# One TensorE block for a unit's gate products, and wider planned margins for float64 conversions

## The chip, the cores and the metric

The kernel runs on one core of a Trainium2 chip, in one launch. The metric is the device time of that launch in microseconds (us). Engines are named as in the profile: PE is TensorE (PEld its weight loads), DVE is VectorE, ACT is ScalarE, POOL is GpSimd, and SP is SyncE, which here only issues DMA transfers. Every engine works through its own instructions strictly in the order in which they were written; an instruction that has to wait holds up all that stand behind it on that engine.

## What is computed

Three computations follow each other. The first is an attention with a window of 16 positions and, beside it, one summary key (a maximum) and one summary value (a mean) for each block of 32 positions. The second is a mixture of 8 experts with a fixed capacity, where tokens are given to experts by their sorted gate logits. The third is a bilinear feed-forward network. The reference, cut to what matters:

```python
q, k, v: (4, 8, 768, 64)                       # float32
scores = [where(|i-j| < 16, q k^T / 8, -1e9),  q k_blockmax^T / 8 + log 32]
x = softmax(scores) @ [v, v_blockmean]         # -> x: (3072, 512)

logits = x @ w_gate                            # (3072, 8): the gate
# tokens go to experts in order of falling logits, 384 tokens to each expert
h = maximum(x[mask_e] @ w1[e], 0);  x[mask_e] = h @ w2[e]      # 8 experts

out = (((x @ wa) * (x @ wb)) @ w3) @ w_out     # wa, wb: (512, 1024); w3: (1024, 1024)
```

The weights wa, wb, w3 and w_out of the third part arrive as float64, of which the chip's engines read the two 32-bit halves; everything else is float32.

## The kernel before

**Stages.** In the attention stage, 16 units (a batch element and two heads each) are worked off with three groups each, 48 groups in all. A group makes scores on PE, subtracts the maximum (DVE, POOL), takes the exponential (ACT), transposes (PE), multiplies with the values (PE) and normalises (DVE). Its output `xo` is transposed on PE and copied by ACT to a tile `xt` of 128 x 256, and `xt` is multiplied with the gate weights `wg` (the gate product, PE, 32 output rows into a quarter of the PSUM tile `rt`, L755 to L763). Four units of a batch element add up in one `rt`; its sum is copied to `lt`, transposed and put into the logits `LG` (L764 to L771). Beside this work, the attention stage converts w_out and w3. When the last logits are there, the routing of expert 0 starts, which is a search in six rounds on DVE with small matmuls on PE (`key`, `gq`, `need`, `base`), and the products w3 x w_out are made on PE (`fold`: `ac<-wh,xh` and the like). After that come the 8 experts, about 93 us each; expert 0's stretch also converts wa and wb and holds the routing of expert 1. An expert has four layers: l1 and l2 are the expert's two matrices, l3 the bilinear products with wa and wb (`ab` tiles), l4 the product with the folded matrix.

**A conversion.** `conv` (L564 to L582) turns 128 x 512 float64 numbers into float32. SP loads them into `st` (one of two buffers, 512 KB) or, for the first halves of wa and wb, into an `ab` tile. Then ACT takes the magnitude of the high words (`a<-st`) and converts the low words in place (`st<-st`); DVE does three instructions (two TENSOR_SCALAR `a<-a`, one SCALAR_TENSOR_TENSOR `a<-st,a`); POOL adds (`a<-a,st` or `w<-a,st`), and with that the `st` buffer is free again. For w_out, ACT and POOL then split the result into `wh` and `wl`; for wa and wb, ACT and POOL split it into two `ab` tiles. There are 40 conversions: 24 are due in the attention stage, 8 in expert 0's routing, 8 in the beginning of expert 0.

**What sets the order.** The kernel isn't written in the order in which it runs. Class `Plan` (L100 to L323) records every instruction with its engine, its due time (`with at(t)`) and an estimated duration, and `Plan.run` (L221 to L323) lists them engine by engine: it goes forward in an estimated time, and whenever an engine is free it takes the ready instruction with the earliest due time. An instruction is ready when its operands are done, plus a margin where they come from another engine: 200 ns in general (SAFE_O), 1200 ns when PE reads them (SAFE_A), and 1500 ns more behind a DMA load (SAFE_D). Instructions recorded after the attention's buffers are given up (`late`; the 16 conversions of wa and wb among them) get no margin, save 600 ns for PE. The margins are not in the program that runs; they only push an instruction further back in its engine's order. `with nc.block()` makes several PE instructions one entry of the plan, so that nothing is put between them. Otherwise every instruction is an entry of its own, and PE's entries are chosen with a malus when the array's tiling changes (PEN, SWITCH); a gate product uses 128 rows by 32 columns of the array, most of its neighbours all 128 columns.

Before the change, gate products are recorded singly, each with its own operands; those of units 0 and 1 of a batch element are recorded together after unit 1, those of units 2 and 3 after unit 3, for the last batch element unit by unit and at last group by group. All recorded code runs through L380, so line numbers say little, and instructions are told apart by their tiles.

Of the kernel before, what the change touches and what calls it, by code (L numbers as in the profile page):

```python
# [99 lines left out]
class Plan:  # L100
# [3 lines left out]
    def __init__(self, nc):  # L104
        self.nc, self.ops, self.base, self.t, self.hot = nc, [], 0, 0.0, False
        self.hots, self.dma = set(), 0.0
        self.gate, self.bar, self.late = None, None, []
        self.rings, self.free, self.done, self.last, self.grabbed = {}, {}, {}, {}, ()
        self.clock, self.ctx = 0.0, nullcontext
        self.parts, self.modes, self.mode = None, {}, None  # L110
        for e in ("tensor", "vector", "scalar", "gpsimd", "sync"):
            setattr(self, e, Engine(self, e))
# [7 lines left out]
    @contextmanager  # L120
    def urgent(self):

        self.hot, old = True, self.hot
        yield
        self.hot = old

    @contextmanager
    def low_precision(self, reason):
# [22 lines left out]
    def add(self, eng, fn, reads, writes, dur, post):  # L151
        i = len(self.ops)
        deps, bufs = {}, []
        for v, wr in [(v, False) for v in reads] + [(v, True) for v in writes]:
            b = v.buf
            for j, kj, wj in b.seen:
                if j != i and (wr or wj) and overlap(v.key, kj):
                    deps[j] = max(deps.get(j, 0), 2 if wj and not wr else 1)
            if b not in bufs:
                bufs.append(b)  # L160
                b.uses += 1
        for v, wr in [(v, False) for v in reads] + [(v, True) for v in writes]:
            if not v.buf.seen or v.buf.seen[-1] != (i, v.key, wr):
                v.buf.seen.append((i, v.key, wr))
        for v in self.grabbed:
            bufs.append(v.buf)
            v.buf.uses += 1
        self.grabbed = ()
        if self.gate is not None:
            deps.setdefault(self.gate, 0)  # L170
        if any(b.pool is p for b in bufs for p in self.late if len(p) < 1 or b.n > 1):
            deps.setdefault(self.bar, 0)
        new = [b for b in bufs if not b.held]
        for b in bufs:
            if b.held and b.first is not None:
                deps.setdefault(b.first, 0)
        for b in new:
            b.held, b.first = True, i
            if b.fifo:
                if b.ring in self.last:  # L180
                    deps.setdefault(self.last[b.ring], 0)
                self.last[b.ring] = i
        deps.pop(i, None)
        if self.hot:
            self.hots.add(i)
        self.ops.append((eng, fn, deps, bufs, new, self.t, dur, post))

    def whole(self, tile, shape):
# [32 lines left out]
    def run(self):  # L221
# [22 lines left out]
        while todo:  # L244
            moved = False
            for e, (wait, q) in ready.items():
# [42 lines left out]
                for j in users.get(i, ()):  # L289
                    kind = ops[j][2][i]  # L290
                    if kind == 0:
                        settle(i, j, t)
                    else:
                        late = self.bar is not None and j > self.bar
                        safe = 0.0
                        if e != ops[j][0] and not late:
                            safe = SAFE_A.get(ops[j][0], SAFE_O) + (SAFE_D if post else 0.0)
                        elif e != "tensor" and ops[j][0] == "tensor":
                            safe = SAFE
                        settle(i, j, done + safe + (0.0 if post else LAG[e].get(ops[j][0], 0.0)))  # L300
            if moved:
                continue
# [27 lines left out]
       "gpsimd": {"tensor": 143, "scalar": 76, "vector": 80, "sync": 240}}  # L330

HOLD = 150.0

SWITCH, PEN = 150.0, 3.0

# [96 lines left out]
def body(tc, q, k, v, w_gate, w1, w2, wa, wb, w3, wo, out):  # L432
# [131 lines left out]
    def conv(src, r, h, dst, t, raw=None):  # L564

        with at(t - P_CL):
            raw = stage() if raw is None else raw
            nc.sync.dma_start(raw.bitcast(I32), src[r * 128:(r + 1) * 128, h * 512:(h + 1) * 512].bitcast(I32))
        with at(t):
            w = raw.bitcast(I32).rearrange("p (a b) -> p a b", b=2)  # L570
            lo, hi = w[:, :, 0], w[:, :, 1]
            c = ep.tile([128, 512], F32, name="a", bufs=3)
# [12 lines left out]
    for j in range(FB):  # L585
        t = P_C0 + (T0 - P_C1) * j / nconv
        f = conv(wo, j, 0, None, t)
        with at(t):
            WO[j] = wu()
            split_sb(WO[j][0], WO[j][1], f)  # L590
            for x in WO[j]:
                nc.keep(x)
# [99 lines left out]
    def group(G):  # L692
# [59 lines left out]
            nc.scalar.activation(xt, ps, AF.Copy)  # L752
            XT[u, g] = xt

        last = b == B - 1 and pr == HP - 1  # L755
        for x in ([(u, g)] if last else [(y, i) for y in (u - 1, u) for i in range(3)] if g == 2 and (pr == 1 or pr == 3)
                  else [(u, i) for i in range(3)] if g == 2 and b == B - 1 and pr == 2 else []):
            with at(STEP * G + P_SC):
                y, i = x
                if y % HP == 0 and i == 0:  # L760
                    GT[b] = pp.tile([128, 256], F32, name="rt", fifo=True)
                nc.tensor.matmul(GT[b][32 * i:32 * i + 32], WG[:, y % HP], XT[x].rearrange("p t s -> p (t s)"),
                                 start=(y % HP == 0), stop=(y % HP == HP - 1))  # L763
        if pr == HP - 1 and g == 2:  # L764
            with at(STEP * G + P_SC):
                lt = ap_.tile([96, 256], F32, name="lt", bufs=1)
# [499 lines left out]
```

## Time and profile before

| | us |
|---|---|
| median of 3 runs | 1042.55 |
| lowest and highest | 1041.95, 1046.04 |
| the profiled execution | 1044.22 |
| its span, first to last instruction | 1042.4 |
| PE busy (share of the span) | 955.7 (92%) |
| DVE busy | 662.1 (64%) |
| ACT busy | 406.1 (39%) |
| POOL busy | 322.4 (31%) |

The profiled execution lies 1.7 us over the median, and 1.8 us of it lie outside its span. The busy shares are averages over stages that are limited by different things, so they have to be read by stage: a table of stretches gives each engine's busy time, PE's granted clock and the DMA engines' share. What an engine waited for stands in a list of waits (summed), in the timeline (each instruction with the idle time before it in brackets), and in the chain of waits, which goes back from the last instruction and at each step to what released it.

### The profile page before, as it was taken

Reading aid. Unit: us, or ns where it says so; the run is one execution under the profiler, and the core shown is the slowest. Engines: PE = TensorE matmul, PEld = TensorE weight load, DVE = VectorE, ACT = ScalarE, POOL = GpSimd, SP = SyncE. Lnnn points to the kernel's source line nnn. Section 1 sums busy time; section 2 is a strip of 40 time slices with the busy share of each in tenths; the row PEclk is TensorE's granted clock in tenths of the full one; section 3 lists DMA queues with packets and bytes.
Section 4 is the critical chain, followed back from the end, with each engine's and each line's share of the span. In section 5 each row is a group of like instructions: output and inputs, shape, how many; then the busy total and the mean of one; then the engine's idle time right before and its main releaser. Section 6 shows DMA issues by size and latency. Waiting matters only on the chain.

```text
span 1042.4 us, 17312 instructions
## 1 busy us (share of the span) xinstructions
PE 955.7 (92%) x6339; PEld 847.5 (81%) x6339; DVE 662.1 (64%) x1992; ACT 406.1 (39%) x845; POOL 322.4 (31%) x393
## 2 busy tenths in 40 slices
PE   5799977997688899999999999999999999999995
PEld 4577766765477789979988997998899799999994
DVE  6989978879978972882686288258628825423210
ACT  4778866745244333232323323232332323323211
POOL 8877757525613631030121103012110304101001
PEclk9999999999889899999999999999999999999998
DMA  8999987570323331040113105011310405101000
GB/s 222 222 262 237 227 207 185 149 246 1 129 66 99 121 105 58 1 162 11 52 66 98 60 2 162 11 51 66 98 60 1 162 11 172 41 11 51 1 1 31
DMA packets 84007, 102.12 MB, mean 98 GB/s; under 512 B 31185, under 2 KB 64465, under 8 KB 83921
## 3 DMA queue, kind: packets, MB, share of 16 engines
q1 hardware_dynamic: 70864, 54.86, 19.7%
q0 software_dynamic: 13056, 46.14, 13.4%
q8 instruction: 50, 0.82, 0.3%
q14 instruction: 37, 0.30, 0.1%
HBM read 86.00 MB, written 12.58 MB: 95 GB/s over the span
## 4 chain that ended last, share of the span: by engine, by line
PE 61%; DVE 17%; issue 11%; DMA 6%; ACT 3%; SPq 1%; POOL 1%; POOLq 0%; DVEq 0%; ACTq 0%
PE mm L380 35%; PE ac L380 24%; DVE a L380 4%; DVE gq L380 2%; PE rt L380 2%; DMA st<-in_moe_w_dram 2%; DVE s L380 1%; DMA qn<-in_q_dram 1%; SPq L380 1%; DMA vn<-in_v_dram 1%; DVE xl L380 1%; DMA vw<-in_v_dram 1%; DMA st<-in_moe_w_out_dram 1%; DVE wl L380 1%; DVE kw L380 1%
## 5 line engine op out<-in xcount | busy, mean ns | idle before, releaser
L380 PE MATMUL mm<-xh,ab 128*128 128x384 f32 x1024 | 275.8, 341 | 0.0
L380 PEld LDWEIGHTS mm<-xh,ab 128*128 128x128 f32 x1024 | 188.4, 190 | 4.2 <-issue 2.6
L380 PE MATMUL mm<-xl,ab 128*128 128x384 f32 x512 | 175.7, 343 | 1.9 <-DVE xl L380 1.9
L380 DVE TENSOR_TENSOR a<-a,mm 128x384 f32<-128x384 f32 x64 | 35.3, 551 | 143.5 <-PE mm L380 120.9
L380 PE MATMUL ac<-w,hh 128*128 128x512 f32 x384 | 124.6, 400 | 0.0
L380 PEld LDWEIGHTS mm<-xl,ab 128*128 128x128 f32 x512 | 97.2, 190 | 4.7 <-DVE xl L380 3.2
L1056 POOL DMA_INDIRECT ra<-in_moe_w_dram,iw x32 | 31.7, 991 | 200.3 <-DVE go L380 190.9
L380 ACT ACTIVATE a<-mm 128x384 f32<-128x384 f32 x64 | 31.4, 491 | 147.3 <-PE mm L380 130.5
L380 PE MATMUL mm<-xh,wh 128*128 128x384 f32 x256 | 88.0, 345 | 0.4 <-ACT xh L380 0.4
L380 PE MATMUL ac<-hl,wh 128*128 128x384 f32 x256 | 87.1, 340 | 0.0
L380 PE MATMUL mm<-xl,wh 128*128 128x384 f32 x256 | 86.9, 339 | 0.0
L380 PE MATMUL mm<-xh,wl 128*128 128x384 f32 x256 | 86.8, 339 | 0.0
L380 PE MATMUL ac<-hh,wl 128*128 128x384 f32 x256 | 86.5, 338 | 0.0
L380 PE MATMUL ac<-hh,wh 128*128 128x384 f32 x256 | 84.1, 337 | 0.0
L1118 POOL DMA_INDIRECT out_dram<-a,idx x24 | 26.7, 1113 | 176.9 <-ACT a L380 173.6
L380 DVE TENSOR_TENSOR wl<-st,wh 128x512 fp32r<-128x512 f32 x64 | 45.5, 711 | 56.1 <-ACT wh L380 55.8
L380 PEld LDWEIGHTS ac<-w,hh 128*128 128x128 f32 x384 | 70.8, 188 | 11.6
L380 ACT ACTIVATE hh<-a 128x384 fp32r<-128x384 f32 x64 | 33.6, 525 | 119.3 <-DVE a L380 117.2
L1056 POOL DMA_INDIRECT xg<-xd,idx x24 | 25.3, 1054 | 167.4 <-PE mm L380 128.2
L380 PE MATMUL ac<-w,hl 128*128 128x512 f32 x192 | 76.6, 399 | 0.0
L380 ACT ACTIVATE wh<-ra 128x512 fp32r<-128x512 f32 x64 | 41.9, 666 | 65.5 <-PE mm L380 30.7
L380 DVE TENSOR_TENSOR wl<-ra,wh 128x512 fp32r<-128x512 f32 x64 | 43.9, 688 | 31.7 <-ACT wh L380 31.7
(253 smaller groups left out, 2096.2 us busy)
## 6 DMA issues: line engine op xcount, KB each, us to landing
st<-in_moe_w_dram SPq DMA_DIRECT2D x24, 512.0 KB, 3.9
kn<-in_k_dram SPq DMA_DIRECT2D x32, 192.0 KB, 4.8
qn<-in_q_dram SPq DMA_DIRECT2D x32, 192.0 KB, 4.1
vn<-in_v_dram SPq DMA_DIRECT2D x8, 768.0 KB, 9.2
xd<-xo SPq DMA_DIRECT2D x48, 128.0 KB, 4.1
vw<-in_v_dram SPq DMA_DIRECT2D x32, 176.0 KB, 4.7
st<-in_moe_w_out_dram SPq DMA_DIRECT2D x8, 512.0 KB, 5.2
ab<-in_moe_w_dram SPq DMA_DIRECT2D x8, 512.0 KB, 8.0
```

The costliest lines, as they stand in the source:

```text
L380: return getattr(real_engine, method)(*map(real, a), **{k: real(x) for k, x in kw.items()})
L1056: nc.add("gpsimd", lambda: tc.nc.gpsimd.indirect_dma_start(out=real(dst), out_offset=None, in_=real(src), in_offset=bass.IndirectOffsetOnA ...
L1118: s = tc.nc.gpsimd.indirect_dma_start(out=out, out_offset=bass.IndirectOffsetOnAxis(ap=real(idx), axis=0), in_=real(o), in_offset=None)
```

## The change

It has three parts. (1) A unit's three gate products are recorded as one block after its third group, for every unit, and so is the accumulation over the four units; no unit is paired with another any more. (2) `nc.patient()` marks instructions, those of SP excepted; `conv` uses it for its six instructions behind the load, and the split of w_out for its two. (3) For a marked instruction the planner's margin behind another engine is at least 1000 ns (CALM), and behind a DMA load 3500 ns (CALM_D); for instructions recorded after the attention's buffers are given up it is 0.3 of that, 300 and 1050 ns.

```diff
@@ Plan.__init__
+        self.calm, self.calms = False, set()
@@ class Plan
+    @contextmanager
+    def patient(self):
+
+        self.calm, old = True, self.calm
+        yield
+        self.calm = old
@@ Plan.add
+        if self.calm and eng != "sync":
+            self.calms.add(i)
@@ Plan.run, where an instruction i is done and its user j becomes ready
                         elif e != "tensor" and ops[j][0] == "tensor":
                             safe = SAFE
+                        if j in self.calms and e != ops[j][0]:
+                            safe = max(safe, (CALM_D if post else CALM) * (0.3 if late else 1.0))
                         settle(i, j, done + safe + (0.0 if post else LAG[e].get(ops[j][0], 0.0)))
@@
+CALM, CALM_D = 1000.0, 3500.0
@@ conv, behind its load
-        with at(t):
+        with at(t), nc.patient():
@@ the split of w_out
-        with at(t):
+        with at(t), nc.patient():
             WO[j] = wu()
@@ group
-        last = b == B - 1 and pr == HP - 1
-        for x in ([(u, g)] if last else [(y, i) for y in (u - 1, u) for i in range(3)] if g == 2 and (pr == 1 or pr == 3)
-                  else [(u, i) for i in range(3)] if g == 2 and b == B - 1 and pr == 2 else []):
+        if g == 2:
             with at(STEP * G + P_SC):
-                y, i = x
-                if y % HP == 0 and i == 0:
+                if pr == 0:
                     GT[b] = pp.tile([128, 256], F32, name="rt", fifo=True)
-                nc.tensor.matmul(GT[b][32 * i:32 * i + 32], WG[:, y % HP], XT[x].rearrange("p t s -> p (t s)"),
-                                 start=(y % HP == 0), stop=(y % HP == HP - 1))
+                with nc.block():
+                    for i in range(3):
+                        nc.tensor.matmul(GT[b][32 * i:32 * i + 32], WG[:, pr], XT[u, i].rearrange("p t s -> p (t s)"),
+                                         start=(pr == 0), stop=(pr == HP - 1))
```

No instruction is added or taken away; the change moves them. From the middle of expert 0's third layer on the orders of all engines are the same before and after: the last 3787 of PE's 4995 entries other than gate products, and on DVE the last 964 of 1770. Three places follow. In the orders, `wg` are the gate weights, `xt` a group's transposed output, numbers tell buffers apart, and the new code's line is L394 where the old one's is L380.

PE near the end of the attention stage, before: the gate products of the last unit but one, with transposes (`ident`) between them.

```order
L380 MATMUL rt_2949<-xt_3066,wg_352 32x256
L380 MATMUL ac_3106<-ident_86,s_3043 120x128 x4
L380 MATMUL mm_3118<-ident_86,w_0_1726 128x128 x2
L380 MATMUL mm_3124<-ident_86,xo_3095 128x128 x2
L380 MATMUL mm_3118<-ident_86,w_0_1726 128x128 x2
L380 MATMUL mm_3132<-ident_86,w_0_1726 128x128 x3
L380 MATMUL rt_2949<-xt_3104,wg_352 32x256
L380 MATMUL mm_3132<-ident_86,w_0_1726 128x128
L380 MATMUL ac_3147<-ident_86,s_3078 120x128 x4
L380 MATMUL ac_3154<-vw_0_122,pt_0_134 64x65 x8
L380 MATMUL rt_2949<-xt_3140,wg_352 32x256
```

The same three products after the change:

```order
L394 MATMUL ac_3151<-ident_86,s_3081 120x128 x4
L394 MATMUL ac_3143<-wh_493,xl_3067 128x512
L394 MATMUL rt_2888<-xt_3026,wg_350 32x256
L394 MATMUL rt_2888<-xt_3114,wg_350 32x256
L394 MATMUL rt_2888<-xt_3139,wg_350 32x256
L394 MATMUL ac_3163<-vw_0_122,pt_0_211 64x65 x8
L394 MATMUL ac_3143<-wh_741,xh_3066 128x512
```

Three single products have become three in a row, and PE changes its tiling once for them instead of three times. Over the whole stage the 48 products stood at 37 places and now stand at 16.

ACT in the middle of the attention stage, before: the twelfth and the thirteenth conversion (`a<-st`, then `st<-st`), among copies of scores and transposes.

```order
L380 ACTIVATE kw_0_117<-mm_2231 128x5x16
L380 ACTIVATE vs_0_120<-mm_2229 64x2x64
L380 ACTIVATE a_2289<-st_2173 128x512
L380 ACTIVATE s_2235<-s_2235 128x480
L380 ACTIVATE pt_0_211<-ac_2283 120x512
L380 ACTIVATE st_2173<-st_2173 128x512
L380 ACTIVATE xt_2328<-mm_2312 128x256
L380 ACTIVATE a_2336<-st_2221 128x512
```

The twelfth conversion on ACT after the change:

```order
L394 ACTIVATE kw_0_117<-mm_2321 128x5x16
L394 ACTIVATE kw_0_117<-mm_2321 128x6x16
L394 ACTIVATE qb_0_94<-mm_2333 64x6x64
L394 ACTIVATE a_2367<-st_2215 128x512
L394 ACTIVATE pt_0_323<-ac_2342 120x512
L394 ACTIVATE st_2215<-st_2215 128x512
L394 ACTIVATE s_2338<-s_2338 128x480
L394 ACTIVATE vs_0_120<-mm_2325 64x2x64
L394 ACTIVATE xt_2401<-mm_2387 128x256
```

It stands six rows further back in the engine's order, and the thirteenth conversion, five rows behind it before, now stands seventeen rows behind it.

DVE at the end of the routing of expert 1, before: `i` and `idx` are its last results, on which PE and the gathers wait; the last conversion (not shown) ends thirteen rows ahead of this piece.

```order
L380 TENSOR_TENSOR hl_4826<-a_4766,hh_4802 128x384
L380 TENSOR_SCALAR tk_4756<-tk_4756 128x24
L380 TENSOR_TENSOR LG_1278<-LG_1278,tk_4756 128x192
L380 TENSOR_TENSOR LG_1278<-LG_1278,pe_4700 128x192
L380 COPY i_0_4852<-rt_4788 128x6
L380 TENSOR_REDUCE key_4854<-LG_1278 128x24
L380 SCALAR_TENSOR_TENSOR idx_4862<-i_0_4852 128x3
L380 TENSOR_TENSOR rem_559<-rem_559,rt_4856 128x8
```

The same place after the change:

```order
L394 COPY i_0_4799<-rt_4739 128x6
L394 SCALAR_TENSOR_TENSOR a_4697<-st_4618,a_4697 128x512
L394 SCALAR_TENSOR_TENSOR idx_4807<-i_0_4799 128x3
L394 TENSOR_TENSOR rem_623<-rem_623,rt_4803 128x8
L394 TENSOR_TENSOR LG_1347<-LG_1347,pe_4656 128x192
L394 SCALAR_TENSOR_TENSOR rem_623<-es_4650,rem_623 128x8
L394 TENSOR_TENSOR a_4769<-a_4769,mm_4766 128x384
L394 TENSOR_SCALAR a_4773<-a_4773 128x512
L394 TENSOR_REDUCE key_4825<-LG_1347 128x24
L394 TENSOR_SCALAR a_4773<-a_4773 128x512
L394 TENSOR_TENSOR hl_4834<-a_4769,hh_4821 128x384
L394 SCALAR_TENSOR_TENSOR a_4773<-st_4680,a_4773 128x512
```

The last three conversions end here or behind it, where they had been ahead of it: ten instructions that stood ahead of `idx` now stand behind it, six of them of the last two conversions, one product `a<-a,mm` with its `hl`, and two small ones of the routing.

## Rows read from the trace of the kernel before

**Rows 1.** Stretches of the span: attention, routing 0, begin of expert 0, rest.

```profile
core 0: us, PE busy (x) PEld busy (x) DVE busy (x) ACT busy (x) POOL busy (x), PEclk, DMA share, GB/s
0.00:219.00 219.00, 183.94 (x1809) 142.01 (x1810) 179.62 (x647) 154.04 (x373) 154.70 (x222) 0.99 0.83 214
219.00:284.00 65.00, 48.01 (x278) 34.38 (x279) 62.52 (x147) 27.33 (x49) 34.31 (x26) 0.98 0.33 112
284.00:370.40 86.40, 71.41 (x400) 64.13 (x399) 72.51 (x191) 34.89 (x63) 33.94 (x27) 0.88 0.32 101
370.40:1042.40 672.00, 652.37 (x3855) 606.95 (x3854) 347.45 (x1011) 189.83 (x361) 99.43 (x119) 0.99 0.18 58
```

**Rows 2.** Three stretches of the attention stage, columns as in rows 1.

```profile
52.00:78.00 26.00, 24.26 (x255) 18.67 (x256) 23.14 (x80) 19.30 (x47) 19.53 (x25) 0.93 0.95 262
...
130.00:156.00 26.00, 20.92 (x228) 17.09 (x226) 20.35 (x73) 17.57 (x45) 14.06 (x18) 1.00 0.83 208
...
182.00:219.00 37.00, 34.70 (x329) 25.46 (x330) 26.16 (x101) 25.30 (x56) 16.61 (x15) 1.00 0.58 168
```

**Rows 3.** DVE's waits, 0 to 216 us: total, times, longest.

```profile
DVE a L380 <- ACT a L380: 9.2, 6, 3.0
...
DVE rs L380 <- PE ac L380: 4.1, 7, 0.9
DVE s L380 <- PE ac L380: 3.9, 4, 1.6
```

**Rows 4.** ACT's waits for the w3 loads, 0 to 216 us.

```profile
ACT a L380 <- DMA st<-in_moe_w_dram: 6.1, 5, 2.3
```

**Rows 5.** DVE's timeline: four conversions; in brackets idle time before, and releaser.

```profile
147.41 0.43 DVE L380 TENSOR_SCALAR a<-a 128x512 f32<-128x512 f32 x1 [3.04 <-ACT a L380]
...
151.11 1.04 DVE L380 TENSOR_SCALAR a<-a 128x512 f32<-128x512 f32 x1 [0.66 <-ACT a L380]
...
171.44 0.89 DVE L380 TENSOR_SCALAR a<-a 128x512 f32<-128x512 f32 x2 [2.23 <-ACT a L380]
...
174.63 1.50 DVE L380 TENSOR_SCALAR a<-a 128x512 f32<-128x512 f32 x1 [0.89 <-ACT a L380]
```

**Rows 6.** The chain of waits at two loads of w3: start, us, what.

```profile
141.11 5.58 DMA st<-in_moe_w_dram
...
168.07 5.83 DMA st<-in_moe_w_dram
```

**Rows 7.** DVE's timeline, begin of expert 0: first and last of four conversion waits.

```profile
316.43 0.43 DVE L380 TENSOR_SCALAR a<-a 128x512 f32<-128x512 f32 x1 [0.63 <-ACT a L380]
...
358.60 0.97 DVE L380 TENSOR_SCALAR a<-a 128x512 f32<-128x512 f32 x1 [0.60 <-ACT a L380]
```

**Rows 8.** The chain of waits: gate products on it (two records each).

```profile
47.12 0.56 PE rt L380 x6
...
201.82 0.55 PE rt L380 x2
...
215.78 0.55 PE rt L380 x2
```

**Rows 9.** All gate products, grouped by line: busy us, mean ns, idle before.

```profile
L380 PE MATMUL rt<-xt,wg 128*32 128x256 f32 x96 | 23.8, 396 | 0.0
```

**Rows 10.** The chain where PE's idle times end: l3, l4, l3.

```profile
370.55 2.90 PE mm L380 x16
373.45 2.09 PE ac L380 x9
375.54 4.16 PE mm L380 x24
```

**Rows 11.** DVE's timeline: third DVE instruction of the last conversion.

```profile
360.06 0.69 DVE L380 SCALAR_TENSOR_TENSOR a<-st,a 128x512 int32<-128x512 int32 x1
```

**Rows 12.** The chain of waits, begin of expert 0: a load of wa or wb.

```profile
320.18 4.33 DMA st<-in_moe_w_dram
```

**Rows 13.** POOL's timeline: the addition of a conversion of wa or wb.

```profile
318.26 1.30 POOL L380 TENSOR_TENSOR a<-a,st 128x512 int32<-128x512 int32 x1 [13.56 <-DVE a L380]
```

## The prediction

> **What bounds the kernel now.** I read the table of stretches first, then the waits of each engine, then the chain of waits. The stretches [rows 1] show three regimes. From 370.4 us on PE is busy 652.37 of 672.00 us, and there the order is not touched: whatever the change gives or costs must lie ahead of about 370 us and is carried to the end as a shift. In the routing of expert 0 and the beginning of expert 0, from 219 to 370.4 us, DVE is busy 135.0 of 151.4 us, and PE waits for it. In the attention stage, up to 219 us, no engine is full: PE 183.94, DVE 179.62. Within it [rows 2] PE and DVE are close to full from 52 to 78 us (24.26 and 23.14 of 26), with the DMA engines at 0.95; from 130 to 156 us both fall to about 20.5 of 26 with the DMA engines at 0.83, so something is waited for there that is not throughput; from 182 to 219 us PE is full again, 34.70 of 37.
>
> The waits say what. DVE sat idle 9.2 us for a conversion's magnitude from ACT, six times [rows 3], and ACT 6.1 us for the loads of w3 [rows 4]. Four of DVE's six waits, 3.04, 0.66, 2.23 and 0.89 us, lie between 147 and 175 us [rows 5], and right ahead of them the chain of waits runs through two loads, 5.58 and 5.83 us [rows 6]. Conversions are needed only after the attention, so an engine that stops for one there stops the attention for nothing.
>
> **The conversions in the attention stage.** The change adds and removes no instruction and no wait; it puts the conversion's instructions further back. ACT's first one is planned 3500 ns behind its load, where it was 200 + 1500; DVE's is planned 1000 ns behind ACT, where it was 200. A wait of DVE that stems from a late load thus shrinks by up to 1.8 + 0.8 = 2.6 us, another by 0.8. The four waits, 6.8 us, would come down to 0.44 (3.04 less 2.6) and about nothing: 6.4 us less on DVE, at a place where the chain runs through the loads. The other two of the six waits (2.4 us together) would lose 1.6, but they lie where the chain goes elsewhere, and I count nothing. Value 6.4 us, bounds 3 (the two longer ones half cured) and 8.0.
>
> What is queued behind these instructions gains; what is queued behind the conversion's end may lose: POOL's addition frees the `st` buffer, and SP issues the next load of w3 after it, with loads of q, k and v behind that one. SP's instructions are not marked, but they were moved along, since the plan frees the buffer later. I count nothing for that, because the conversions stand some 8 us apart with two buffers between them.
>
> **The conversions at the beginning of expert 0.** Four more waits of DVE, the first 0.63 and the last 0.60 us [rows 7], 2.7 us in all, stand on the DVE that bounds this stretch. The margins there go from nothing to 300 ns, and from nothing to 1050 behind a load. I count 2.1 us, bounds 0 and 2.7.
>
> **Work that changes sides.** Ten DVE instructions leave the place ahead of `idx` of expert 1, after which PE is never idle again [rows 10]: three DVE instructions of each of two conversions (0.43 twice and 0.69, [rows 7, 11], so 3.1 us), and a product, its `hl` and two small ones, which I put at 1.4 together. So routing 1 could be over 4.5 us earlier. But the conversions still have to be done: the last one's product is read by PE in l3 of the fifth column block. Before, DVE was through with it at 360.75 [rows 11], and PE came there at 375.54 [rows 10]. Now the last but one ends some 3.5 us behind `idx`, at about 370.5 - 4.5 + 3.5 = 369.5. From there: POOL gets to its addition behind gathers (some 2 us) and adds (1.30, [rows 13]): 372.8; the freed buffer is loaded again (4.33, [rows 12]): 377.1; the last conversion follows with ACT 0.7, DVE 1.5, POOL 1.3, ACT 0.6, POOL 1.3 and about 0.8 of hand-overs: 383.3, its first half at about 381.4. PE, released 4.5 us earlier, ends the fourth l3 block at 368.9 (373.45 less 4.5), does l4 (2.09), 21 of 24 products of l3 (3.65) and the l4 that the plan has put ahead of the late ones (2.09), and wants the first half at 377. It waits about 4.1 us. Net 0.4 us gained of 4.5; bounds 4.5 gained (POOL and the load come through faster) and 3 lost. So the margin's own price nearly eats this gain.
>
> **The gate products.** A single product holds PE for 0.55 us, and six records, three products in three quarters of the array's columns, for 0.56 [rows 8]: three run beside each other. The 48 products, 23.8 us of records [rows 9], stood at 37 places: 37 x 0.55 = 20.4 us; 16 blocks take 16 x 0.56 = 9.0. PE has 11.4 us less to do. What of it counts: between 199 and 217 us, where PE is full, six single products lie on the chain, from the one at 201.82 to the one at 215.78 [rows 8], 3.3 us, and two blocks remain, 1.1: 2.2 us less. Between 51 and 86 us eight places lie on the chain (4.4 us) and three blocks would stand there (1.7): 2.7 less, but DVE is at 23.14 of 26 there [rows 2]. Of the 4.9 I count half, 2.5 us, bounds 0 and 4.9. The last block comes no later than the last single product: both wait for the same last `xt`, and both take 0.55.
>
> The Trainium skill ("TensorE: Matmul & The Clock Gate", Packing small matmuls, measured speedup) gives three column tiles 2.38 times the rate of one and not 3. By it a block would take 0.69 us and PE's work fall by 9.4 us instead of 11.4; the row at 47.12 us speaks for 3.
>
> **The sum.** 6.4 + 2.1 + 0.4 + 2.5 = 11.4 us. It is a sum of cures, and the reordering moves every engine's instructions in this stage by some five places; a DVE that comes earlier waits longer for PE, as it did for 4.1 and 3.9 us in eleven waits [rows 3]. I let a third come back as other waits, by no row of its own: 7.6 us. The profiled execution took 1044.22 us (span 1042.4 and 1.8 around it), 1.7 above the median; from its time the sum gives 1036.6, from the median, with which the new time will be compared, 1034.9. I say 1035. With the lower bounds of all terms (3 + 0 - 3 + 0) it would be 1042.5, with the upper ones (8.0 + 2.7 + 4.5 + 4.9 = 20.1) 1022.4.
>
> **Rivals.**
> *The freed time is taken by other waits.* For it: between 52 and 78 us DMA, PE and DVE are all over 0.88 busy [rows 2]. Against it: the longest conversion waits lie after 140 us, where none is. Then only a fifth of the 11.4 us arrives, 2.3: 1040.3.
> *Slower: the last conversion holds up expert 0.* The place is the chain of loads worked out above: each of the last conversions needs the `st` buffer of one before, and the margins have put them behind the routing. If neither the stage gains nor the routing ends earlier, and the two last loads run one after the other, there is one more round of load (4.3) and conversion (6.2) in the way: the product is ready at 383.3 + 10.5 = 393.8, where PE wants it at 379.2 (375.54 and 21 products of 0.174) and can put l4 of 2.1 before it. PE waits 12.5 us: 1055. It decides from the point at which the product is ready later than 381.3, that is, when the last load is issued later than about 371 us. Shorter waits of the kind give 1048.
> *More: the clock recovers too.* In the beginning of expert 0 PE's granted clock is 0.88 on average [rows 1], and a granted clock has two levels, 1.2 and 2.4 GHz: a quarter of 86.4 us, some 21 us, at the lower one, which costs 10.4 us of array time, after PE had waited for DVE. If PE waits less there, half of that may go, 5 us more: 1030; with the whole 4.5 us of the routing 1025.5. The Trainium skill (same page, the HAM clock gate) says that the throttled state is the default and that activity releases it, which agrees with a clock that is lower only where PE waits.
> *The change does not do what it says* is settled by the order: products and conversions did move.
>
> **How the numbers follow.** Forecast 0.50 (1031 to 1039 around 1035), freed time taken 0.26 (1038 to 1044), slower 0.10 (1046 to 1055), clock 0.14 (1024 to 1031). Telling from no change takes about 0.5% here, 5.2 us: faster means under 1037.3. Of the forecast seven tenths lie under it (0.35), of the clock all (0.14), of the second rival a fifth (0.06): 0.55 faster; the rest of the two, 0.35, is no change, 0.10 slower. The range reaches from the clock's case, 1025, to the end of the second rival, 1044; the slower case is left out, and some 0.05 below.
>
> **What would show it.** In the new profile: DVE's waits for ACT's `a` in the attention stage, 9.2 us, should be under 3; single gate products should be gone and PE's busy time lower by about 11 us up to 219 us; the first `key` should come some 6 to 8 us earlier; PE should show an idle time of 0 to 5 us at the last `ab` tiles of expert 0. The rest, from there to the end, should take as long as before. I would be wrong if SP's waits for POOL grow and loads of q, k and v come late, or if PE's new wait in l3 is longer than 5 us.

## The result, and the profile after

The changed kernel took 1033.26 us, median of 4 runs (1028.42 to 1035.59), against 1044.1 of the kernel before (4 runs, 1041.95 to 1046.04): ratio 0.9891, 95% interval 0.9847 to 0.9934. Measured once more, beside other runs of before (1040.89 us, median of 14; experiments, below), it was 0.9925 (0.9900 to 0.9950). So it is 8 to 11 us faster; 7.6 were predicted. Each experiment's ratio is to the runs of before on its own chip.

The stretches of [rows 1], in the first profile of the changed kernel; borders as there: 0.4 us behind the last logits, behind `idx` of expert 0, at `idx` of expert 1.

```profile
core 0: us, PE busy (x) PEld busy (x) DVE busy (x) ACT busy (x) POOL busy (x), PEclk, DMA share, GB/s
0.00:212.60 212.60, 176.69 (x1806) 146.97 (x1807) 169.12 (x640) 150.05 (x366) 146.07 (x220) 0.94 0.83 211
212.60:281.60 69.00, 50.57 (x277) 36.55 (x276) 65.44 (x149) 29.35 (x52) 31.19 (x24) 0.88 0.36 128
281.60:357.50 75.90, 64.96 (x388) 57.16 (x387) 68.93 (x185) 31.85 (x58) 28.08 (x23) 0.93 0.35 108
357.50:1033.80 676.30, 656.17 (x3873) 609.99 (x3872) 359.58 (x1021) 194.26 (x369) 110.04 (x127) 0.99 0.18 59
```

The first two in its second profile (the others are 75.90 and 676.30 again):

```profile
0.00:207.90 207.90, 173.18 (x1806) 143.98 (x1807) 169.53 (x640) 150.11 (x366) 147.42 (x220) 0.97 0.82 216
207.90:276.50 68.60, 50.49 (x278) 36.27 (x277) 65.44 (x149) 29.36 (x52) 30.23 (x24) 0.88 0.36 128
```

Beside 219.0, 65.0, 86.4 and 672.0 before: the attention is 6.4 and 11.1 us shorter, routing 0 some 4 longer, the beginning of expert 0 10.5 shorter, the rest 4.3 longer. **Two executions of one order differ by 4.7 us in the attention stage**, so a stage of a single profile is not read closer than that below, unless it repeats.

DVE's waits in the attention stage, first profile after (0 to 212 us), beside [rows 3]:

```profile
DVE vr L394 <- DMA vn<-in_v_dram: 10.7, 4, 4.0
DVE rs L394 <- PE ac L394: 8.1, 10, 2.0
DVE s L394 <- PE ac L394: 5.2, 8, 1.0
...
DVE a L394 <- ACT a L394: 3.7, 3, 1.6
```

The same list of the kernel before has this row for the loads of v:

```profile
DVE vr L380 <- DMA vn<-in_v_dram: 4.7, 3, 3.1
```

The conversion waits fell from 9.2 to 3.7 us, and three other waits rose by 11.3. Up to the last logits DVE stood idle 39.4 us before (218.6 less 179.2 busy), 43.4 and 38.3 after (212.2 less 168.8, 207.5 less 169.2). It doesn't wait less; **it has 10 us less to do there**. DVE's groups for the conversions up to the last logits (instructions, then busy us and mean ns), before:

```profile
L380 DVE SCALAR_TENSOR_TENSOR a<-st,a 128x512 int32<-128x512 int32 x21 | 17.9, 853 | 0.1
...
L380 DVE TENSOR_SCALAR a<-a 128x512 f32<-128x512 f32 x22 | 12.7, 577 | 9.3 <-ACT a L380 9.2
L380 DVE TENSOR_SCALAR a<-a 128x512 int32<-128x512 int32 x21 | 12.6, 600 | 0.3
```

and in the second profile after:

```profile
L394 DVE SCALAR_TENSOR_TENSOR a<-st,a 128x512 int32<-128x512 int32 x19 | 15.7, 825 | 0.2
...
L394 DVE TENSOR_SCALAR a<-a 128x512 f32<-128x512 f32 x19 | 11.5, 605 | 3.4 <-ACT a L394 3.2
L394 DVE TENSOR_SCALAR a<-a 128x512 int32<-128x512 int32 x19 | 10.9, 576 | 0.2
```

Two conversions have left the stage (seven instructions, with the rest's shorter times 43.2 to 38.1 us); the other 5 us are instructions that are as many and run shorter. This is bookkeeping: neither DVE nor PE was full in this stage, and it doesn't say which of them held it up.

PE's share: all gate products, grouped, after ([rows 9] before: 23.8).

```profile
L394 PE MATMUL rt<-xt,wg 128*32 128x256 f32 x96 | 10.1, 391 | 0.0
```

Counted from each record's start to the next instruction's start or its own end, they held PE for 20.5 us before and 9.1 and 8.9 after; 20.4 and 9.0 were predicted. What counts is the last quarter, from the third to the fourth batch element's logits, where PE is full. Before, and in the second profile after:

```profile
181.60:218.60 37.00, 34.68 (x328) 25.44 (x328) 25.94 (x101) 25.30 (x56) 16.77 (x16) 1.00 0.58 166
```

```profile
175.80:207.50 31.70, 29.21 (x315) 23.27 (x315) 24.20 (x96) 22.45 (x50) 14.99 (x15) 1.00 0.50 148
```

It is 5.3 us shorter, the same in the first profile (31.8), and PE's work fell by as much: 2.6 us are gate products; 1.2 of score products and 0.7 of transposes of w3 now stand elsewhere.

### The profile page after: what moved, and what is told of

It is laid out like the page before. It is cut to its first block, busy times and chain, and to the rows that moved or that the text cites. A ratio compares the mean times of both kernels' runs of the same rounds, so it can differ in the third digit from the quotient of the medians.

```text
span 1033.8 us, 17299 instructions
## 1 busy us (share of the span) xinstructions
PE 948.4 (92%) x6339; PEld 850.7 (82%) x6339; DVE 663.1 (64%) x1992; ACT 405.5 (39%) x845; POOL 315.4 (31%) x393
## 4 chain that ended last, share of the span: by engine, by line
PE 59%; DVE 14%; issue 13%; DMA 7%; ACT 3%; POOL 2%; SPq 1%; POOLq 0%; ACTq 0%; DVEq 0%
PE mm L394 32%; PE ac L394 25%; DVE a L394 3%; DMA ra<-in_moe_w_dram,iw 3%; DMA vn<-in_v_dram 2%; SPq L394 1%; DVE gq L394 1%; PE rt L394 1%; DVE wl L394 1%; POOL ra L1069 1%; DVE xl L394 1%; DVE s L394 1%; DMA vw<-in_v_dram 1%; DVE base L394 1%; ACT wh L394 1%
## 5 line engine op out<-in xcount | busy, mean ns | idle before, releaser
L394 PE MATMUL mm<-xh,ab 128*128 128x384 f32 x1024 | 276.2, 340 | 2.0 <-ACT ab L394 2.0
L394 PEld LDWEIGHTS mm<-xh,ab 128*128 128x128 f32 x1024 | 186.5, 189 | 10.8 <-issue 6.0
L394 PE MATMUL mm<-xl,ab 128*128 128x384 f32 x512 | 175.0, 342 | 0.0
L394 DVE TENSOR_TENSOR a<-a,mm 128x384 f32<-128x384 f32 x64 | 35.3, 551 | 139.5 <-PE mm L394 117.0
L394 PE MATMUL ac<-w,hh 128*128 128x512 f32 x384 | 123.9, 400 | 0.1
L394 PEld LDWEIGHTS mm<-xl,ab 128*128 128x128 f32 x512 | 96.6, 189 | 5.2 <-issue 2.5
L394 PE MATMUL mm<-xh,wh 128*128 128x384 f32 x256 | 87.4, 342 | 0.6 <-DVE xl L394 0.6
L394 PE MATMUL ac<-hl,wh 128*128 128x384 f32 x256 | 87.1, 340 | 0.3 <-DVE hl L394 0.3
L394 PE MATMUL ac<-hh,wl 128*128 128x384 f32 x256 | 86.7, 339 | 0.0
L394 PE MATMUL mm<-xh,wl 128*128 128x384 f32 x256 | 86.5, 338 | 0.0
L394 PE MATMUL mm<-xl,wh 128*128 128x384 f32 x256 | 86.4, 337 | 0.0
L394 ACT ACTIVATE a<-mm 128x384 f32<-128x384 f32 x64 | 31.4, 490 | 139.7 <-PE mm L394 139.7
L394 PE MATMUL ac<-hh,wh 128*128 128x384 f32 x256 | 84.4, 337 | 0.0
L394 PEld LDWEIGHTS ac<-w,hh 128*128 128x128 f32 x384 | 70.8, 189 | 12.0 <-ACT hh L394 0.4
L394 ACT ACTIVATE hh<-a 128x384 fp32r<-128x384 f32 x64 | 33.6, 525 | 117.6 <-DVE a L394 117.6
L394 DVE TENSOR_TENSOR wl<-st,wh 128x512 fp32r<-128x512 f32 x64 | 44.5, 696 | 53.4 <-ACT wh L394 53.2
L394 PE MATMUL ac<-w,hl 128*128 128x512 f32 x192 | 76.0, 396 | 0.0
L394 DVE TENSOR_TENSOR wl<-ra,wh 128x512 fp32r<-128x512 f32 x64 | 50.1, 785 | 36.2 <-ACT wh L394 36.2
L394 PE MATMUL ac<-kw,qb 128*128 128x120 f32 x384 | 65.3, 299 | 6.6 <-DVE mx L394 6.5
```

The costliest lines, as they stand in the source:

```text
L394: return getattr(real_engine, method)(*map(real, a), **{k: real(x) for k, x in kw.items()})
```

## The experiments

**Each part alone.** Blocks without marks, and marks without blocks:

```diff
-        if self.calm and eng != "sync":      # e1: the gate blocks of after, no instruction marked
-            self.calms.add(i)
```
```diff
-                with nc.block():             # e2: gate products as before, instructions marked
+        for x in ([(u, g)] if last else [(y, i) for y in (u - 1, u) for i in range(3)] ...
```

> The gate products as blocks, no instruction marked, so all margins as before. Theory (conversion margins carry the gain, gate products a small part of it): 2.5 us less than the kernel before, bounds 0 and 4.9, ratio 0.998; DVE's waits for the conversions' magnitude in the attention stage stay near the 9.2 us in six of the kernel before; PE's busy time some 11 us lower. Rival one (the blocks carry the gain, since PE loses 11 us of work): 8 to 11 us less, ratio 0.990 to 0.992, whatever the conversion waits are. Rival two (each new order of the attention stage is a new throw, and neither part has a price of its own): anything from 5 us less to 5 us more.

> The margins of the changed kernel, the gate products singly and paired as before. Theory: the conversion waits of DVE in the attention stage fall from 9.2 us to under 4, the first logits of expert 0 are complete some 4 to 6 us earlier, the whole is 6 to 9 us shorter, ratio 0.991 to 0.994. Rival one (the blocks carry the gain): 0 to 1 us shorter, ratio 0.999 to 1. Rival two (a new throw): anything between 5 us less and 5 us more, and not the sum of the two parts.

Measured: blocks 0.9956 (0.9940 to 0.9972), 4.6 us less; margins 0.9944 (0.9922 to 0.9966), 5.8 less. Together 10.4, about the whole. Blocks alone fall short of it; for margins alone that isn't shown, since their interval overlaps the 0.9900 to 0.9950 of the changed kernel's second measurement. Their attention stages, blocks first (an execution of 1045.2 us, 5 over their median):

```profile
0.00:216.00 216.00, 172.49 (x1810) 139.96 (x1811) 180.70 (x646) 154.02 (x372) 152.67 (x222) 0.98 0.82 213
```

```profile
0.00:217.00 217.00, 181.74 (x1809) 141.70 (x1810) 173.65 (x640) 150.90 (x368) 149.96 (x220) 0.98 0.82 213
```

The blocks take work from PE (11 us), the margins from DVE (6 us), and the engine relieved stood idle longer for it. The last logits came at 215.6 and 216.6 us, only 3.0 and 2.0 earlier than before; for the margins 4 to 6 were expected. The rest of their gain lies behind: from the last logits to `idx` of expert 2 their kernel took 236.7 us, the kernel before 241.9. Conversion waits fell in both (5.5 us in six, where 9.2 were expected to stay; 3.5 in four): for losing a good part of them no margin was needed, only another order.

**How far do orders scatter?** The kernel before with 300 ns for 200 as the general margin; the changed kernel with 100 ns more; and that without margins for the late conversions (wa and wb):

```diff
-SAFE_A, SAFE_O, SAFE_D = {"tensor": 1200.0, "sync": 2000.0}, 200.0, 1500.0
+SAFE_A, SAFE_O, SAFE_D = {"tensor": 1200.0, "sync": 2000.0}, 300.0, 1500.0    # e9
-CALM, CALM_D = 1000.0, 3500.0
+CALM, CALM_D = 1100.0, 3600.0                                                 # e4, e8
-                        if j in self.calms and e != ops[j][0]:
+                        if j in self.calms and e != ops[j][0] and not late:   # e8
```

> The kernel before, with the general margin of 300 ns in place of 200 for everything in the attention stage (gate products singly, no instruction marked): its conversions gain 0.1 us of margin per hand-over, its order is another. Theory (the gain of the changed kernel is that of its mechanisms): within 3 us of the kernel before, ratio 0.997 to 1.003, conversion waits of DVE still over 6 us. Rival (orders scatter, and the order before was an unlucky one): 4 us or more shorter than the kernel before, with conversion waits still there.

> The changed kernel with margins of 1100 and 3600 ns in place of 1000 and 3500: no mechanism of the prediction changes by more than 0.1 us per conversion, and the planned order of the attention stage is a different one in places. Theory: within 2 us of the changed kernel, 8 to 12 us under the kernel before, conversion waits of DVE under 4 us. Rival (each order is a new throw, and the gain of the changed kernel is partly luck): 3 us or more away from the changed kernel, with waits of other kinds in other places.

> Margins of 1100 and 3600 ns in the attention stage and none for the late conversions (wa and wb): the kernel that was 1042.1 us with margins for these too, while its logits were complete 7.3 us earlier than in the kernel before. Theory (its loss of 8 us on the changed kernel arose in expert 0, where PE waited for gathers and ab tiles, and the attention's gain is real): 1031 to 1036 us, ratio 0.987 to 0.992, no wait of PE for xg or ab in expert 0. Rival (the loss came from the attention's own order, a new throw): still 1039 to 1044 us.

Measured: 0.9991 (0.9971 to 1.0010); 0.9969 (0.9948 to 0.9989); 0.9942 (0.9921 to 0.9964). A new order of the kernel before, without a cure, moved nothing, with waits as long as ever (0 to 221 us):

```profile
DVE a L380 <- ACT a L380: 12.1, 9, 4.1
```

But 100 ns more of margin left 3 of the 8 to 11 us. The theory for the third kernel missed, and so did its rival: 1036.2 us lies between the two. Leaving the late margins out gave back no more than 3 us, and PE still waited for a gather in expert 0, as it had before the change (4.6 us):

```profile
PE mm L394 <- DMA xg<-xd,idx: 4.3, 1, 4.3
```

Part of the loss lies in the attention's own order, the rival's case: the last quarter took 33.6 us in both kernels with 1100 ns, against 31.3 to 31.8 in five profiles of the changed kernel's order. The last logits (211.3 and 211.9 us) say no more, since those of that one order scatter from 207.2 to 212.2. A tenth of margin thus costs 5 to 8 us with the late margins (0.9891 and 0.9925 against 0.9969) and 4 to 7 without (0.9880 and 0.9907, below, against 0.9942). What the neighbours keep is 3 and 6 us; of the 8 to 11 us, 2 to 8 hang on this one order.

**Do late loads cost what the prediction said?** The 24 loads of w_out and w3 cut to an eighth, in the order of before (e11) and of after (e12). The conversions read this eighth again and again, in as many instructions of the same sizes; seven eighths of the two matrices are left out. The edit in short:

```diff
-            nc.sync.dma_start(raw.bitcast(I32), src[r * 128:(r + 1) * 128, h * 512:(h + 1) * 512]...)
+            nc.sync.dma_start(raw.bitcast(I32)[:, 0:128], src[r * 128:(r + 1) * 128, h * 512:h * 512 + 64]...)
```

> The kernel before, in the same order, but each of the 24 loads of w_out and w3 brings an eighth of its bytes (64 KB of 512), and the conversion reads those again and again; its instructions are as many and of the same sizes, and what they compute of w_out and w3 is wrong. So no conversion waits for its load, at the old margins, and no other load stands behind these. Theory (the conversions' waits for late loads hold up the attention, the margins cure them): DVE's waits for the conversions' magnitude fall from 9.2 us to under 3 and ACT's for st to none, and the kernel is 5 to 9 us shorter than the kernel before, ratio 0.991 to 0.995. Rival one (these waits are beside the path, the margins' gain was another order): within 2 us of the kernel before. Rival two (all loads of the stage are what holds it up, those of q, k and v too): more than 12 us shorter.

> The changed kernel with the same small loads of w_out and w3, in its own order. Theory (its margins have already taken out what late loads of w_out and w3 cost): 0 to 3 us shorter than the changed kernel, so that the two kernels with small loads lie only 3 to 6 us apart, by the blocks alone. Rival one (its waits for q, k and v, 10.7 us of DVE for vn, come from the traffic of these loads): 5 us or more shorter than the changed kernel. Rival two (the gain is another order): the two kernels with small loads lie as far apart as the two with full loads, 8 us or more.

Measured: 0.9949 (0.9931 to 0.9967), 5.3 us less than before; 0.9873 (0.9850 to 0.9896), 5.4 less than the changed kernel beside it. The third quarter, in which the prediction had put 6.4 us; before, then before with small loads:

```profile
130.00:181.60 51.60, 40.95 (x441) 32.58 (x439) 42.29 (x153) 35.02 (x88) 33.03 (x41) 1.00 0.77 198
```

```profile
133.50:178.50 45.00, 40.44 (x440) 32.48 (x439) 42.05 (x152) 34.58 (x88) 33.90 (x41) 1.00 0.65 165
```

6.6 us less in the same order with the same work. The four waits of [rows 5] fell from 6.8 to 2.0 us, and the quarter's 1.5 us of waits for v went too; over the stage the conversion waits fell from 9.2 to 4.2, where under 3 was expected. Two of the four, 3.04 and 2.23 us before, here:

```profile
147.23 0.43 DVE L380 TENSOR_SCALAR a<-a 128x512 f32<-128x512 f32 x1 [0.60 <-ACT a L598]
...
169.26 1.07 DVE L380 TENSOR_SCALAR a<-a 128x512 f32<-128x512 f32 x2 [0.77 <-ACT a L598]
```

But the changed kernel gains as much from small loads (5.4 us, 1.9 to 8.9), its conversions' waits unchanged at 3.2 us, and the two kernels with small loads lie 7.9 us apart (0.0076, 0.0047 to 0.0105), as far as with full ones: rival two. **Over the whole kernel the change has not taken the loads' cost away.** In the third quarter most of it has gone. The quarter took 46.5 and 46.1 us after, and with small loads:

```profile
127.80:171.60 43.80, 38.02 (x431) 32.53 (x432) 37.52 (x146) 33.06 (x82) 28.52 (x39) 0.96 0.71 174
```

Full loads cost 2.3 to 2.7 us there, where it had been 6.6. No margin was needed for that: blocks alone had the quarter in 46.9 us, margins alone in 49.3. Nor do the loads of v bear what the conversions' loads cost, as rival one has it. In the second and third quarter DVE's waits for `vn` grew from 1.5 us to 6.0 and 6.9, but with small loads they are still 5.5, and over the stage (0 to 203 us) 9.2, for 9.9 in the second profile with full ones:

```profile
DVE vr L394 <- DMA vn<-in_v_dram: 9.2, 4, 3.4
```

So these waits came with the new order, and for the most part not from the traffic of w_out and w3. Where else the 5.4 us lie, one profile doesn't show: the first quarter took 81.9 us with small loads, and from 83.7 to 88.7 in five profiles with full ones.

**The changed kernel again, and its late margins.** As e8's third edit, on the changed kernel (twice), and the whole margin for late conversions (`* 1.0` for `0.3 if late`):

> The changed kernel once more, for a narrower interval and a second profile in the same order. If the single profile of it is representative: ratio 0.985 to 0.993, logits of the last batch element complete at 211 to 213 us. If the attention stage of one order scatters from execution to execution by the clock and the loads (the two variants with the same order up to there had them at 207.2 and 208.8 us): 206 to 210 us, and a ratio of 0.988 to 0.993.

> The changed kernel, but the conversions recorded after the attention's buffers are given up (the first eight of wa and wb in routing 0, the last eight in expert 0) get no margin, as before the change. Theory (the late margins give back in l3 of expert 0 what they gain in routing 1): the attention's gain stays, idx of expert 1 comes some 4 us later than in the changed kernel, PE doesn't wait for the last ab tiles in l3, and the whole is within 2 us of the changed kernel. Rival one (the late margins are what makes routing 1 early, and that carries): 3 to 5 us longer than the changed kernel. Rival two (the late margins only cost): 2 to 4 us shorter than the changed kernel.

> The changed kernel without margins for the late conversions once more, beside the changed kernel on the same chip: theory (the late margins are worth nothing, or cost a little) the same within 2 us or up to 3 us shorter; rival (they are worth the 2.1 us of waits that they were to cure) 2 us or more longer.

> The changed kernel, but the late conversions (wa and wb) get the whole margin, 1000 ns and 3500 behind a load, not 0.3 of it. The order of the attention stage is the same up to its end. Theory (the late margins move conversions behind the routing's results, and give it back where PE waits for the last ab tiles in l3 of expert 0): routing 1 is done earlier still or as early, PE's wait there grows from 2.0 us to 4 to 8, and the whole is 2 to 6 us longer than the changed kernel, ratio to the kernel before 0.991 to 0.995. Rival (the late margins cure waits of DVE, and more margin is as good): within 2 us of the changed kernel, PE's wait there not over 3 us.

Measured: the changed kernel 0.9925; without late margins 0.9880 (0.9853 to 0.9908), the second time 0.9907 (0.9884 to 0.9931), 1 to 2 us under the changed kernel, which the intervals don't separate: no gain by the late margins shows. With whole ones 0.9928 (0.9903 to 0.9953), no different from the changed kernel's 0.9925, so the 2 to 6 us of the theory didn't show. PE's waits there came mostly from another tile than `ab` (340 to 400 us):

```profile
PE mm L394 <- DVE xl L394: 4.7, 1, 4.7
...
PE mm L394 <- POOL ab L394: 1.0, 2, 0.7
```

`idx` of expert 1 came at 346.9 us there, at 361.4 and 361.2 without late margins, and the spans are 1031.7, 1030.4 and 1026.6. Being 14 us early at that point was worth nothing: at `idx` of expert 2 it was 5 to 6 us, and from there to the end this kernel took 589.4 us, the others 582.5 and 579.6.

Without late margins routing 0 took 63.0 and 63.1 us, with them 69.0 and 68.6. Part of the reason stands on POOL. Second profile after, POOL and DVE:

```profile
264.59 1.27 POOL L394 TENSOR_TENSOR ab<-a,ab 128x512 fp32r<-128x512 f32 x1
265.81 2.53 POOL L394 TENSOR_TENSOR a<-a,ab 128x512 int32<-128x512 int32 x2
268.30 2.48 POOL L394 TENSOR_TENSOR ab<-a,ab 128x512 fp32r<-128x512 f32 x2
```

```profile
264.54 6.35 DVE L394 TENSOR_TENSOR R<-hi,cid 128x72 bf16<-128x72 f32 x1
```

In the first profile after it was another instruction of the same search, while POOL did the same five (270.00 to 276.19):

```profile
269.40 7.62 DVE L394 TENSOR_TENSOR gq<-iof,lo 128x768 bf16<-128x768 bf16 x1
```

`R` takes 0.24 us in that profile and `gq` 0.95. This order had put five POOL instructions of conversions behind each other, and DVE, which bounds this stretch, stood until they were through, 6.1 and 6.7 us. Before, POOL did two in a row there and an instruction of DVE took 2.78 us for 0.17; the difference, 3.5 to 4, is as much as routing 0 grew by. Without late margins POOL did three, with a gap, and DVE lost 3.3 us there in three pieces. The rows show the stop; that it is the price of late margins they don't show. Routing 0 took 62.8 us with margins alone and 63.1 with whole late margins, and 68.5 with blocks alone, where no instruction is marked and a `gq<-iof,lo` of 4.97 us met four instructions of POOL in a row. It is the order again.

**PE's time put back.** Two products more behind each block, into an unused quarter of `rt`, order otherwise unchanged (the edit in short):

```diff
+                    for i in range(2):
+                        nc.tensor.matmul(GT[b][96:128], WG[:, pr], XT[u, i]..., start=True, stop=True)
```

> The changed kernel in the same order; behind each of the 16 blocks of gate products PE does two more products of 32 columns into the unused fourth quarter of the PSUM tile rt. They are not part of the computation and nothing reads them. The first can run beside the block, the second lasts 0.55 us: 0.55 to 1.1 us a block, 9 to 18 us more work for PE in the attention stage, about what the blocks had taken away (11.4). Theory (PE's time counts there at the share of the prediction, 2.5 of 11.4): 2 to 4 us longer than the changed kernel. Rival one (PE's time counts in full, the blocks carry the gain): 9 to 18 us longer. Rival two (PE's time there is hidden): within 1 us of the changed kernel; then the gain of the blocks alone was that of another order.

Measured: 0.9945 (0.9923 to 0.9967), 2.1 us over the changed kernel's 0.9925 (1.4 under to 5.5 over). They held PE for 6.9 us more (15.8 for 8.9), less than expected. The last quarter grew by 0.6 us:

```profile
177.60:209.90 32.30, 30.77 (x330) 23.98 (x329) 24.31 (x96) 22.37 (x50) 15.43 (x15) 1.00 0.50 148
```

A microsecond of PE costs about 0.3 here, with zero not excluded; the full 6.9 us, rival one's price, is excluded.

## Why the prediction was right, step by step

The size was right, and so was the place: ahead of `idx` of expert 2 the kernel gained 6.9 and 11.6 us, behind it 1.7 and 2.1 (581.9 before, 580.2 and 579.8 after), and kernels whose orders agree there scatter from 579.6 to 582.6. Several steps behind the size were not right, so the size is in good part luck: its largest term failed on the mechanism, and a tenth more margin, which changes no term by more than 0.1 us per conversion, left 3 us of the gain.

- **Conversions in the attention, 6.4 us.** Their price was about right: with small loads the third quarter lost 6.6 us, 4.8 of them these waits and 1.5 waits for v. The step that failed is that the margins cure it. Margins alone brought the last logits 2.0 us earlier, and blocks alone shortened the third quarter nearly as much as the whole change (46.9 us against 46.5 and 46.1; 51.6 before). There the conversion waits did fall, but DVE's idle time didn't (9.3 us before, 10.1 and 8.8 after); work had gone from the quarter. The prediction took margins as a cure for waits; they are a later place in a list, and two conversions went out of the stage.
- **Conversions at the beginning of expert 0, 2.1 us.** The waits of [rows 7], 2.7 us in four, were gone after; without late margins there was one of 1.1 us in the first profile and none in the second, so the margins needn't be the reason. Missed was routing 0, some 4 us longer with POOL's run in front of DVE, which gave it back nearly twice over: the sum has no term for POOL's instructions in front of DVE.
- **Work that changes sides, 0.4 us net.** Routing 1 became not 4.5 but 10.6 us shorter (from `idx` to `idx`, 87.0 to 76.4 us), and the next one 6 longer. PE's waits at the late tiles (281 to 400 us, where 4.1 was foreseen):

```profile
PE mm L394 <- ACT ab L394: 2.0, 1, 2.0
PE ac L394 <- DVE xl L394: 2.0, 1, 2.0
```

  With the term above 2.5 us were foreseen; from the last logits to `idx` of expert 2 it was 241.9 us before and 241.4 in both profiles after, 0.5.
- **Gate products, 2.5 us.** PE's 11.4 us came as 11.4 and 11.6, at 0.56 us a block; the Trainium skill's 2.38 ("TensorE: Matmul & The Clock Gate", Packing small matmuls) would have given 11.0 for what took 8.9. Blocks alone gave 4.6, close to the upper bound of 4.9; the last quarter's share was right for the products themselves (2.6 for 2.2). By the products put back, 0.3 us for one of PE, 11.4 us would be worth 3.4, with zero not excluded; the rest would be the order.
- **A third comes back as other waits.** As much waiting came back, for `vn` and for PE, as had gone. What fell in the stage is work: on DVE two conversions that now stand later and the same instructions run shorter, on PE the gate products. The first rival, that other waits take the freed time, was right on the waits, and its time (1040.3) wrong, since the work changed too.
- **The last conversion, and the clock.** PE's wait in l3 stayed at 2 us, so the slower rival didn't come. The clock recovered at the beginning of expert 0 (0.88 to 0.93) and fell in routing 0 (0.98 to 0.88) and in the attention, so the third didn't either.

Of the signs: conversion waits under 3 us, nearly (3.7, 3.2); PE's work down by 11 us, 183.9 to 173.2 busy in the second profile, hidden by the clock in the first (176.7); the first `key` 6 to 8 us earlier, 6.7 and 11.3. Of the sign of being wrong one half came: SP's waits for POOL did not grow (17.5 us for `w` before, 13.0 and 14.3 after), and yet loads of v came late.

What stays open: why the loads of v are waited for longer, with the same 0.83 of DMA share and with small loads of w_out and w3 as well; how much of the gain is the throw of an order, which its neighbours put at 2 to 8 us; and what shortens the attention stage. Blocks alone took 11 us from PE there and gave 3.0, margins alone took 6 from DVE and gave 2.0, and the two together gave 6.4 to 11.4 in five profiles of one order. That the two reliefs need each other would fit this, but no run separates it from the throw.

## What to carry to other kernels

Before a wait is counted as gained, compare the idle time of that engine over the whole stage, and its work: a margin in a list scheduler is a postponement, and what it pays may not come from the waits for which it was made. Run each part of a change alone, and see whether the waits go without the cure, too. Price a wait by an experiment in the same order (here smaller loads), and a planner's new constant by two or three neighbours of it, since one order is one throw. And when instructions of POOL are moved, look at what DVE does while several of them stand in a row.

## What the runs showed of the hardware

- **A run of POOL instructions can stop a DVE instruction for its whole length**: 6.35 and 7.62 us for instructions of 0.24 and 0.95, ending 0.1 and 0.8 us behind the fifth. The Trainium skill ("SBUF — State Buffer", Who interferes with whom) says that a DVE instruction with two inputs in SBUF and a POOL instruction that reads SBUF exclude each other for an instruction's length. The trace agrees, and shows more: in these two profiles DVE got no turn between five POOL instructions. It isn't always so. With margins alone POOL did five such instructions in a row from 255.02 to 262.47 us, and DVE did one instruction after another meanwhile; one with two inputs waited for the first of the five, another took 1.46 us for 0.95, and POOL's second took 1.72 for 1.27:

```profile
255.17 1.70 DVE L394 SCALAR_TENSOR_TENSOR a<-ab,a 128x512 int32<-128x512 int32 x1
...
258.63 1.46 DVE L394 TENSOR_TENSOR gq<-key,thr 128x768 bf16<-128x768 f32 x1
```

```profile
256.28 1.72 POOL L394 TENSOR_TENSOR ab<-a,ab 128x512 fp32r<-128x512 f32 x1
```

  What decides between the two isn't shown.
- **The granted clock differs between executions of one order.** In the attention stage the same order (the changed kernel's, with or without late margins) had a mean of 0.94, 0.97, 0.98, 0.99 and 1.00 in five profiles, a mixture of 1.2 and 2.4 GHz, and PE busy 176.7, 173.2, 169.9, 169.5 and 167.3 us. The last logits came at 212.2, 207.5, 207.2, 207.9 and 208.8: from the second to the fifth, 5.9 us less of PE's time ended 1.3 later, so at most the first can have been held up by it. What PE did was the same, so no row shows what set it off. The row of the last, with the whole margin for late conversions:

```profile
0.00:209.20 209.20, 167.27 (x1806) 137.42 (x1807) 169.46 (x640) 150.19 (x366) 146.37 (x220) 1.00 0.82 215
```

- **The same DVE instructions take other times in another order, and in another execution of one order**: four `js<-io` of 128 x 31 took 2.5 us before, 1.5 and 0.7 in the two profiles after, and sixteen copies `vw<-vw` 19.7, 18.0 and 17.6, with nothing changed in them.
